# Sparse attention and a capped mixture of experts in one kernel: causal selects queued ahead of folds on GpSimd, gate softmax queued behind the next exponentials, and a new order at the start

## The chip, the cores and the metric

The kernel runs on one core of a Trainium2 chip. The metric is the device time of one execution in microseconds, here the median of three runs. A profiled execution of the same kernel gives the trace.

## The reference

The input is attention for 4 batches of 8 heads, 768 positions and a head width of 64, followed by a mixture of 8 experts over the 3072 x 512 rows that the attention gives.

```python
k_min, k_max = min / max of k over chunks of 32 positions      # 24 chunks
ub = sum_d max(q * k_min, q * k_max)                           # bound per query and chunk
ub = where(own or earlier chunk, ub, -1e9)
sel = chunks that hold the 6 largest ub of the query
scores = where(sel and key <= query, q @ k.T / 8, -1e9)
x = softmax(scores) @ v                                        # heads side by side: 3072 x 512
logits = x @ w_gate;  expert = argmax;  gate = its softmax value
for each of 8 experts: keep the 80 tokens of largest gate that chose it
    out[token] = gate * (relu(x[token] @ w1) @ w2)             # all other rows are zero
```

## The kernel before, in words

The attention works on 16 pairs of heads, four for each batch; all attention matmuls are float32. A small scheduler, `Sync`, records what each operation reads and writes and adds the semaphore waits. Each engine runs its operations in the order in which the program issues them, so the order of the text is the order of five queues: TensorE ("pe"), ScalarE ("act"), VectorE ("dve"), GpSimd ("gp", which also issues the loads of the expert weights) and SP, which issues the other loads and stores.

The main loop at line 633 goes over the pairs. For pair i it issues, in this order: `scores(i)`; at the first pair of a later batch `gate_T` of the batch before; `bounds(i+1)`; `transposes(i+2)`; `values(i)`; `unselT(i+1)`; `rows(i)`; `sums(i)`; `scale_rows(i)`; and, at the last pair of a batch, `gate` and `gate_digits`. Rounds of a top-80 search (`rounds`, a largest-8 search and a removal on VectorE) are scattered between these from pair 4 on.

`transposes` (line 422) turns q and k of a pair with TensorE into the two halves of the score memory SC0 and SC1, copies q and its positive part with ScalarE (qT, rq), copies k with VectorE (kT) and takes the minimum and maximum of each chunk there; GpSimd subtracts them. `bounds` (444) computes the bound of each query and chunk on TensorE and the mask of the chunks that are not selected on VectorE. `unselT` (470) turns that mask.

`scores` (477) goes through six strips of the score matrix, listed in `STEPS`. For a strip TensorE computes the scores and adds the mask, in SC0 and SC1 by turns; ScalarE takes the exponential into EXB (line 497); GpSimd zeroes the entries above the diagonal in the strip's diagonal block (`affine_select`, line 502, called a select here); and GpSimd then folds the strip into ES, a sum over key blocks from which the softmax's denominators are taken (`tensor_tensor`, line 511, called a fold here). The table `ADDS` says which folds follow which strip's select. Before the change strips 1 and 2 have one fold each, strips 3 and 4 three each, strip 5 one. The two selects of strips 4 and 5 therefore stand behind folds in GpSimd's queue.

`values` (514) multiplies the strips with v into OB, in two halves. Its last matmuls in each half need the selects of strips 4 and 5. ScalarE copies OB to oT (526), `rows` (545) turns oT back, and `sums` (528) computes the gate's logits from oT (line 532) and then the denominators from ES (line 537), so this second part needs all folds. `scale_rows` (550) divides and stores the rows.

`gate` (564) reduces the logits of a batch on VectorE, takes one small exponential on ScalarE (line 574) and finishes the softmax and the choice on VectorE (line 582 is its last step). `gate_T` (585) turns the result with TensorE.

Ahead of the loop, lines 355 to 408 issue the first loads and set up constants, among them copies of the gate weights on VectorE (line 407); then `transposes(0)`, `bounds(0)`, `transposes(1)`, `unselT(0)`, with the loads for pairs 2 and 3 between. After the loop follow the last gate, the last search, the choice of slots, and the experts.

Of the kernel before, what the change touches and what calls it, by code (L numbers as in the profile page):

```python
# [17 lines left out]
class Sync:  # L18
# [53 lines left out]
    def op(self, ekey, fn, r=(), w=(), dsem=None, inc=True):  # L72
        is_dma = ekey in self.dma
        stream = self.stream.get(ekey, ekey)
        semkey = dsem if is_dma else ekey
        self.sem(semkey)
        clock = self.clock.setdefault(stream, {})
        need = {}

        def want(ev, same_ok):  # L80
            sk, val = ev
            if sk == ekey and same_ok:
                return
            need[sk] = max(need.get(sk, 0), val)

        for res in r:
            for sk, val in self.lw.get(res, {}).items():
                want((sk, val), ekey == "pe")
        for res in w:
            for sk, val in self.lw.get(res, {}).items():  # L90
                want((sk, val), ekey == "pe")
            for sk, val in self.lr.get(res, {}).items():
                want((sk, val), not is_dma)
        todo = [(sk, v) for sk, v in need.items() if clock.get(sk, 0) < v]

        todo.sort(key=lambda e: -len(self.snaps[e[0]][-1][1]) if self.snaps[e[0]] else 0)
        keep = []
        for i, ev in enumerate(todo):
            implied = False
            for j, other in enumerate(todo):  # L100
                if j == i:
                    continue
                c = {}
                self._learn(c, other)
                if c.get(ev[0], 0) >= ev[1] and not (j > i and self._implied(ev, other)):
                    implied = True
                    break
            if not implied:
                keep.append(ev)
        for ev in keep:  # L110
            assert ev[1] <= self.cnt[ev[0]], (ekey, ev, self.cnt[ev[0]])
            self.queue[ekey].wait_ge(self.sems[ev[0]], ev[1])
        for ev in todo:
            self._learn(clock, ev)
        inst = fn()
        step = 16 if is_dma else 1
        val = self.cnt[semkey] + step
        if inc or is_dma:
            inst.then_inc(self.sems[semkey], step)
            self.cnt[semkey] = val  # L120
            self.snaps[semkey].append((val, dict(clock)))
        for res in w:
            self.lw[res] = {semkey: val}
            self.lr[res] = {}
        for res in r:
            d = self.lr.setdefault(res, {})
            d[semkey] = max(d.get(semkey, 0), val)
        return inst
# [19 lines left out]
def bass_quest_chunk_select__then__topk_capacity_drop_kernel(  # L148
# [26 lines left out]
    def ts(i, n=128):  # L175
# [12 lines left out]
    DIAG = [0, 0, 0, 256, 0, 0]  # L188

    ADDS = [  # L190
        [], [(1, 0, 128, 512)], [(2, 0, 256, 512)], [(3, 0, 512, 768), (3, 256, 512, 768), (1, 384, 512, 640)],
        [(4, 0, 384, 512), (4, 128, 512, 768), (4, 384, 640, 768)], [(5, 0, 640, 768)],
    ]

    FIRST = {(1, 0): (0, 128), (3, 0): (2, 256)}
# [7 lines left out]
    with ExitStack() as pers:  # L203
# [18 lines left out]
        with nc.Block() as blk:  # L222

            @blk.sync
            def _body(_unused):
# [139 lines left out]
                v128 = iv(128, [1, 128])  # L365
                op("gp", lambda: gp.iota(v128, pattern=[[-1, 128]], base=0, channel_multiplier=1), w=["ti"])
                op("dve", lambda: ve.tensor_scalar(ident_f[:], v128, 0, None, ALU.is_equal), r=["ti"], w=["ident_f"])
                for j in range(2):
                    op("dve", lambda: ve.memset(kmm[j][:], 0.0), w=[f"kmm{j}", f"kmd{j}"])
                op("dve", lambda: ve.memset(uns[:], 0.0), w=["uns"])  # L370
# [17 lines left out]
                op("gp", lambda: gp.iota(vr, pattern=[[0, NT], [-1, E]], base=E, channel_multiplier=0),  # L388
                   r=["ti", "ind0", "ind1"], w=["ti"])
                op("dve", lambda: ve.tensor_copy(rank_c[:], vr), r=["ti"], w=["rank_c"])  # L390
                op("dve", lambda: ve.tensor_copy(ident_bf[:], ident_f[:]), r=["ident_f"], w=["ident_bf"])
                op("dve", lambda: ve.memset(ones8[:], 1.0), w=["ones8"])

                vi = iv(128, [1, CAP])
# [7 lines left out]
                op("dve", lambda: ve.tensor_copy(idc[:, :, 0], iv(128, [1, TOKT])), r=["ti"], w=["idc0"])  # L402
                op("gp", lambda: gp.iota(iv(128, [1, TOKT]), pattern=[[0, TOKT]], base=1, channel_multiplier=1), r=["ti"], w=["ti"])
                op("dve", lambda: ve.tensor_copy(idc[:, :, 1], iv(128, [1, TOKT])), r=["ti"], w=["idc1"])
                for h in range(2):
                    pr = slice(h * 64, h * 64 + 64)
                    op("dve", lambda: ve.tensor_copy(wg[pr, :, h * E:(h + 1) * E], wgr[pr, :, :]), r=["wg", f"wgr{h}"], w=[f"wg{h}"])
                WG = ["wg0", "wg1"]

                def wload(e, part):  # L410
# [8 lines left out]
                def pair_of(t, n):  # L419
                    return bass.AP(t, 0, [[2 * n, 128], [n, 2], [1, n]])  # L420

                def transposes(i):
                    s, j = i % NB, i % 2
                    for nm, src, ps in (("qn", qn, 0), ("kn", kn, 1)):
                        for t in range(NT):
                            a = bass.AP(src[s], t * 2 * D, [[2 * NT * D, 128], [1, 2 * D]])
                            op("pe", lambda: pe.transpose(SC[ps][:, ts(t)], a, ident_f[:]),  # L427
                               r=[f"{nm}{s}0", f"{nm}{s}1", "ident_f"], w=[f"SC{ps}"], inc=(t == NT - 1))
                    op("act", lambda: ac.activation(qT[j][:], SC[0][:, 0:S], ACTF.Copy), r=["SC0"], w=[f"qT{j}"])  # L429
                    op("act", lambda: ac.activation(rq[:], SC[0][:, 0:S], ACTF.Relu), r=["SC0"], w=["rq"])  # L430
                    op("dve", lambda: ve.tensor_copy(kT[j][:], SC[1][:, 0:S]), r=["SC1"], w=[f"kT{j}"])
                    kv = bass.AP(kT[j], 0, [[S, 128], [CHUNK, NCH], [1, CHUNK]])
                    op("dve", lambda: ve.tensor_reduce(kmm[j][:, 0, 0:NCH], kv, AX, ALU.min), r=[f"kT{j}"], w=[f"kmm{j}"])
                    op("dve", lambda: ve.tensor_reduce(kmx[:], kv, AX, ALU.max), r=[f"kT{j}"], w=["kmx"])
                    op("gp", lambda: gp.tensor_tensor(kmm[j][:, 1, 0:NCH], kmx[:], kmm[j][:, 0, 0:NCH], ALU.subtract),
                       r=[f"kmm{j}", "kmx"], w=[f"kmd{j}"])

                def stripes(t, off, row, lo, n):

# [145 lines left out]
                def gate_T(b):  # L585
                    for t in range(NT):
                        op("pe", lambda: pe.transpose(OB[0:E, ts(t)], gv[:, b * NT + t, :], ident_f[:]),
                           r=[f"gv{b}", "ident_f"], w=["O0" if t < 4 else "O1"], inc=(t in (3, NT - 1)))
                    op("act", lambda: ac.activation(cand[:, CAP:CAP + S], OB[0:E, 0:S], ACTF.Copy), r=["O0", "O1"], w=["cand"])  # L589
# [34 lines left out]
                        if m < ROUNDS:  # L624
                            top_round(m, False)

                transposes(0)
                load(2, "qk")
                bounds(0)
                transposes(1)  # L630
                load(3, "qk")
                unselT(0)
                for i in range(NP):
                    scores(i)
                    if i % NPB == 0 and i:
                        gate_T(i // NPB - 1)
                    if i + 1 < NP:
                        bounds(i + 1)
                    if i + 2 < NP:
                        transposes(i + 2)  # L640
                    if i + 4 < NP:
                        load(i + 4, "qk")
                    rounds(i, 0, 1)
                    values(i)
                    if i + 2 < NP:
                        load(i + 2, "v")
                    if i + 1 < NP:
                        unselT(i + 1)
                    rounds(i, 1, 2)
                    if i < NP - 1:  # L650
                        wload(i // 2, i % 2)
                    rows(i)
                    sums(i)
                    scale_rows(i)
                    if i % NPB == NPB - 1:
                        gate(i // NPB)
                        if i < NP - 1:
                            gate_digits(i // NPB)
                    rounds(i, 2, 3)
                    if i % 3 == 2 and i < 12:  # L660
                        zk = f"w1_{E - 1}"
                        zr = bass.AP(w1s[E - 1], 0, [[DB * Fd, 128], [1, 2 * Dm]])
                        if i == 2:
                            op("dve", lambda: ve.memset(zr, 0.0), w=[zk])
                        g = i // 3
                        zs = bass.AP(w1s[E - 1], 0, [[DB * Fd, 128], [0, NT], [1, 2 * Dm]]).bitcast(F32)
                        zd = bass.AP(out.tensor, out.offset + g * NT * 128 * Dm, [[Dm, 128], [128 * Dm, NT], [1, Dm]])
                        op("sp", lambda: sp.dma_start(zd, zs), r=[zk], w=[f"outz{g}"], dsem=f"d_zero{g}")


                b = B - 1
                gate_T(b)
                gate_digits(b)
                wload(E - 1, 1)
# [151 lines left out]
```

## Time and profile before

| | |
|---|---|
| runs | 391.44 us median of 3 (391.4 to 392.28) |
| profiled execution | 393.25 us, its span 391.5 us |
| granted TensorE clock, mean | 0.913 |
| TensorE matmul busy | 299.9 us, 77% |
| VectorE busy | 222.6 us, 57% |
| GpSimd busy | 233.0 us, 60% |
| ScalarE busy | 148.5 us, 38% |

The span is the time from the first to the last instruction of the profiled execution, and all times of rows count from its start. The shares are means over stages that differ: the start up to 22 us, sixteen pairs up to 317 us, the last search and the slots up to 358 us, and the experts. In the rows PE is TensorE, PEld its weight loads, ACT ScalarE, DVE VectorE, POOL GpSimd, SP the sync engine; L502 is line 502 of the kernel.

### The profile page before, as it was taken

To read this page: it belongs to the slowest core of one execution; us is meant where nothing else is said; L and a number is where in the kernel's file an instruction comes from. 1 tells how busy PE (TensorE), PEld (TensorE's weight loads), DVE (VectorE), ACT (ScalarE), POOL (GpSimd) and SP (SyncE) were. 2 spreads that over 40 slices of the span, in tenths; PEclk is the share of its full clock that TensorE was granted. 3 is DMA by queue.
4 is the path that set the end of the run, shared out by engine and by line. 5 is a ranking of instruction groups with operands and counts; after the bars stand their busy time and mean duration, and the time that the engine had idled before them with its cause. 6 is when DMAs were issued, how large, how long until landed. Compare 5 with 4: busy or idle time off the path is not lost.

```text
span 391.5 us, 7778 instructions
## 1 busy us (share of the span) xinstructions
PE 299.9 (77%) x3204; PEld 181.5 (46%) x3204; DVE 222.6 (57%) x591; ACT 148.5 (38%) x202; POOL 233.0 (60%) x313
## 2 busy tenths in 40 slices
PE   2198989897888989879989898888979640024994
PEld 2165555454545455546555454545445420014772
DVE  3344244453596776656785865596864058981342
ACT  3064537261735445435636271726434200001220
POOL 4039586685859595939586775768594960005422
PEclk9689999999999999989999999999998885555898
DMA  9843959698578699594989686935556071001121
GB/s 177 146 82 81 167 121 146 129 282 155 102 142 167 102 287 171 103 164 88 192 238 151 128 159 106 264 75 100 82 90 115 14 105 22 1 0 39 46 62 52
DMA packets 104964, 47.50 MB, mean 121 GB/s; under 512 B 88955, under 2 KB 97269, under 8 KB 104928
## 3 DMA queue, kind: packets, MB, share of 16 engines
q1 hardware_dynamic: 89920, 27.94, 30.8%
q0 software_dynamic: 13440, 18.67, 29.6%
q10 hardware_dynamic: 1568, 0.39, 0.5%
q8 instruction: 25, 0.41, 0.4%
q14 instruction: 11, 0.09, 0.1%
HBM read 53.10 MB, written 10.75 MB: 163 GB/s over the span
## 4 chain that ended last, share of the span: by engine, by line
POOL 41%; PE 31%; issue 12%; ACT 6%; DVE 3%; SPq 3%; DMA 1%; POOLq 0%
POOL ES L511 33%; PE SC L486 8%; POOL EXB L502 7%; PE OB L522 5%; ACT EXB L497 5%; PE OB L770 4%; PE OB L547 4%; PE SC L755 3%; PE M L537 3%; SPq L353 2%; PE M L532 2%; PE SC L492 2%; ACT oT L526 2%; PE SC L427 1%; DMA wgr<-in_moe_w_gate_dram 1%
## 5 line engine op out<-in xcount | busy, mean ns | idle before, releaser
L511 POOL TENSOR_TENSOR ES<-ES,EXB 128x256 f32<-128x256 f32 (+1 forms) x112 | 106.9, 961 | 7.8
L486 PE MATMUL SC<-qT,kT 64*128 64x512 f32 (+3 forms) x512 | 98.6, 473 | 8.2 <-ACT EXB L497 6.5
L497 ACT ACTIVATE EXB<-SC 128x1024 f32<-128x1024 f32 x96 | 85.9, 915 | 48.5 <-PE SC L492 46.9
L522 PE MATMUL OB<-EXB,vn 128*64 128x256 f32 (+2 forms) x704 | 81.0, 374 | 22.1 <-POOL EXB L502 22.1
L522 PEld LDWEIGHTS OB<-EXB,vn 128*64 128x64 f32 x704 | 45.9, 141 | 54.9 <-POOL EXB L502 35.0
L486 PEld LDWEIGHTS SC<-qT,kT 64*128 64x128 f32 x512 | 41.7, 190 | 48.3 <-ACT EXB L497 32.2
L511 POOL TENSOR_TENSOR ES<-EXB 128x768 f32<-128x768 f32 (+1 forms) x32 | 49.3, 1541 | 2.7
L526 ACT ACTIVATE oT<-OB 128x512 f32<-128x512 f32 (+1 forms) x32 | 15.7, 490 | 84.0 <-PE OB L522 84.0
L502 POOL TENSOR_SCALAR_AFFINE_SELECT ES<-EXB 128x256 f32<-128x256 f32 x16 | 6.4, 401 | 61.1 <-ACT EXB L497 60.9
L608 DVE MAX8 top<-cand 8x8 f32<-8x848 f32 (+1 forms) x40 | 40.2, 1006 | 1.9 <-ACT cand L589 1.3
L455 DVE STREAM_TRANSPOSE M<-M 128x160 f32<-128x160 f32 x16 | 5.8, 365 | 61.9 <-PE MB L451 61.9
L492 PE MATMUL SC<-unsT,ind 64*128 64x384 bf16 (+3 forms) x256 | 39.3, 300 | 0.0
L502 POOL TENSOR_SCALAR_AFFINE_SELECT EXB<-EXB 128x256 f32<-128x256 f32 x80 | 33.1, 413 | 10.1 <-ACT EXB L497 10.1
L540 DVE STREAM_TRANSPOSE M<-M 128x192 f32<-128x192 f32 x16 | 6.3, 397 | 57.3 <-PE M L537 57.3
L610 DVE MATCH_REPLACE8 cand<-top,cand 8x848 f32<-8x848 f32 (+1 forms) x36 | 35.7, 992 | 0.0
L736 POOL DMA_INDIRECT qn<-x_rows,idx x4 | 3.9, 980 | 36.0 <-issue 36.0
L429 ACT ACTIVATE qT<-SC 128x768 f32<-128x768 f32 x16 | 13.0, 810 | 25.5 <-PE SC L427 25.5
L427 PE MATMUL SC<-ident_f,qn 128*128 128x128 f32 x96 | 15.1, 298 | 8.0 <-DMA qn<-in_q_dram 6.2
L492 PEld LDWEIGHTS SC<-unsT,ind 64*128 64x128 bf16 x256 | 13.1, 96 | 14.5 <-issue 11.3
L427 PEld LDWEIGHTS SC<-ident_f,qn 128*128 128x128 f32 x96 | 11.2, 150 | 12.6 <-issue 10.9
L776 POOL DMA_INDIRECT out_dram<-EXB,idx x8 | 7.4, 921 | 15.9 <-DVE EXB L774 12.9
L747 ACT ACTIVATE rq<-MB 128x320 bf16<-128x320 bf16 x4 | 1.7, 437 | 39.4 <-PE MB L744 39.4
(139 smaller groups left out, 429.0 us busy)
## 6 DMA issues: line engine op xcount, KB each, us to landing
w1s<-in_moe_w_dram POOLq DMA_DIRECT2D x8, 1024.0 KB, 10.1
w2s<-in_moe_w_dram POOLq DMA_DIRECT2D x7, 1024.0 KB, 11.2
qn<-in_q_dram SPq DMA_DIRECT2D x32, 192.0 KB, 3.4
vn<-in_v_dram SPq DMA_DIRECT2D x32, 192.0 KB, 3.9
out_dram<-w1s SPq DMA_DIRECT2D x4, 1536.0 KB, 10.8
kn<-in_k_dram SPq DMA_DIRECT2D x30, 192.0 KB, 3.7
x_rows<-xp SPq DMA_DIRECT2D x16, 192.0 KB, 6.8
EXB<-in_moe_w_dram POOLq DMA_DIRECT2D x1, 1024.0 KB, 9.8
```

The costliest lines, as they stand in the source:

```text
L427: op("pe", lambda: pe.transpose(SC[ps][:, ts(t)], a, ident_f[:]), r=[f"{nm}{s}0", f"{nm}{s}1", "ident_f"], w=[f"SC{ps}"], inc=(t == NT - 1))
L486: op("pe", lambda: pe.matmul(o, kT[j][pr, ts(kt)], qT[j][pr, q0:q1], start=True, stop=False), r=[f"kT{j}", f"qT{j}"], w=[f"SC{s}"], inc=False)
L492: op("pe", lambda: pe.matmul(o, ind[pr, ts(kt)], unsT[j][pr, b0 - 128:q1 - 128], start=False, stop=True), r=[f"ind{h}", f"unsT{j}"], w=[f" ...
L497: op("act", lambda: ac.activation(Ex(st, None, 0, W), src, ACTF.Exp, scale=SCALE), r=[f"SC{s}"], w=[f"E{st}"])
L502: op("gp", lambda: gp.affine_select(ad, a, pattern=[[0, 2], [1, 128]], compare_op=ALU.is_ge, fill=0.0, base=0, channel_multiplier=-1), r=[ ...
L511: op("gp", lambda: gp.tensor_tensor(o, in0, in1, ALU.add), r=[f"E{s2}", f"E{first[0]}"] if first else [f"E{s2}"] + kt, w=kt)
L522: op("pe", lambda: pe.matmul(OB[pr, q0:q1], vn[s][:, kt, h, :], ex, start=(n == 0), stop=last), r=[f"vn{s}{h}", "ES0" if st is None else f ...
L526: op("act", lambda: ac.activation(oT[:, q0:q1], OB[:, q0:q1], ACTF.Copy), r=[f"O{bk}"], w=[f"oT{bk}"])
L547: op("pe", lambda: pe.transpose(OB[:, ts(t)], oT[:, ts(t)], ident_f[:]), r=["oT0", "oT1", "ident_f"], w=[f"O{t // 4}"], inc=(t in (3, NT - ...
L608: op("dve", lambda: ve.max(dst, cv), r=["cand"], w=[f"top{int(last)}{n}"])
L610: op("dve", lambda: ve.match_replace(cv, dst, cv, -2.0), r=["cand", f"top{int(last)}{n}"], w=["cand"])
L770: op("pe", lambda: pe.matmul(o, hTv(e)[:, fb * CAP:(fb + 1) * CAP], w2v(e)[:, fb, :], start=(fb == 0), stop=(fb == FB - 1)), r=[f"hT{s}{fb ...
```

## The change

It has three parts. In `ADDS` the seven folds of strips 3 to 5 are listed with strip 5, so that GpSimd gets the selects of strips 3, 4 and 5 right behind the fold of strip 2, and the seven folds after the last select. `gate` and `gate_digits` of a batch are no longer issued at the end of its last pair, but in the next pair, behind `scores` and ahead of `gate_T`. For the last batch `gate` is issued after the loop.

At the start the bf16 copy of the identity is made earlier, 40 matmuls on it whose result nothing reads are issued on TensorE ahead of the first transposes, `transposes` is split into four functions, the second pair's transposes and its copy of q are issued ahead of the first pair's bounds, and the copies of the gate weights come after `unselT(0)`.

```diff
     ADDS = [
-        [], [(1, 0, 128, 512)], [(2, 0, 256, 512)], [(3, 0, 512, 768), (3, 256, 512, 768), (1, 384, 512, 640)],
-        [(4, 0, 384, 512), (4, 128, 512, 768), (4, 384, 640, 768)], [(5, 0, 640, 768)],
+        [], [(1, 0, 128, 512)], [(2, 0, 256, 512)], [], [],
+        [(3, 0, 512, 768), (3, 256, 512, 768), (1, 384, 512, 640), (4, 0, 384, 512), (4, 128, 512, 768),
+         (4, 384, 640, 768), (5, 0, 640, 768)],
     ]
...
                 op("dve", lambda: ve.tensor_scalar(ident_f[:], v128, 0, None, ALU.is_equal), r=["ti"], w=["ident_f"])
+                op("dve", lambda: ve.tensor_copy(ident_bf[:], ident_f[:]), r=["ident_f"], w=["ident_bf"])
...
-                for h in range(2):
-                    pr = slice(h * 64, h * 64 + 64)
-                    op("dve", lambda: ve.tensor_copy(wg[pr, :, h * E:(h + 1) * E], wgr[pr, :, :]), r=["wg", f"wgr{h}"], w=[f"wg{h}"])
...
-                transposes(0)
+                def warm(n):
+                    for _ in range(n):
+                        op("pe", lambda: pe.matmul(OB[:, 0:128], ident_bf[:], ident_bf[:], start=True, stop=True),
+                           r=["ident_bf"], w=["O0"], inc=False)
+
+                warm(40)
+                turn_q(0)
+                take_q(0)
+                take_r(0)
+                take_k(0)
                 load(2, "qk")
+                turn_q(1)
+                take_q(1)
+                load(3, "qk")
                 bounds(0)
-                transposes(1)
-                load(3, "qk")
+                take_r(1)
+                take_k(1)
                 unselT(0)
+                for h in range(2):
+                    pr = slice(h * 64, h * 64 + 64)
+                    op("dve", lambda: ve.tensor_copy(wg[pr, :, h * E:(h + 1) * E], wgr[pr, :, :]), r=["wg", f"wgr{h}"], w=[f"wg{h}"])
                 for i in range(NP):
                     scores(i)
+                    if i % NPB == 0 and i:
+                        gate(i // NPB - 1)
+                        gate_digits(i // NPB - 1)
                     if i % NPB == 0 and i:
                         gate_T(i // NPB - 1)
...
-                    if i % NPB == NPB - 1:
-                        gate(i // NPB)
-                        if i < NP - 1:
-                            gate_digits(i // NPB)
...
                 b = B - 1
+                gate(b)
                 gate_T(b)
```

`turn_q` holds the transposes of q and k on TensorE, `take_q` and `take_r` the two ScalarE copies of q, and `take_k` the VectorE copy of k, its minima and maxima, and GpSimd's difference.

## Rows read from the trace of the kernel before

**Rows 1.** Page, chain that ended last: shares of the span by engine.
```profile
POOL 41%; PE 31%; issue 12%; ACT 6%; DVE 3%; SPq 3%; DMA 1%; POOLq 0%
```

**Rows 2.** Chain of waits in pair 5, 114 to 133: start us, us, what.
```profile
114.37 1.06 PE SC L486 x4
...
117.82 0.42 POOL EXB L502
...
129.85 0.39 ACT oT L526
...
131.62 0.65 PE M L537 x16
```

**Rows 3.** Timeline, pair 5: start us, us, engine, line, operation, [idle before, its releaser].
```profile
120.64 1.30 ACT L497 ACTIVATE EXB<-SC 128x1024 f32<-128x1024 f32 x2 [0.39 <-PE SC L492]
...
123.24 0.44 PE L522 MATMUL OB<-ES,vn 128*64 128x128 f32 x4
...
126.13 2.60 PE L522 MATMUL OB<-EXB,vn 128*64 128x128 f32 x28 [0.73 <-POOL EXB L502]
...
128.88 0.40 POOL L502 TENSOR_SCALAR_AFFINE_SELECT EXB<-EXB 128x256 f32<-128x256 f32 x1
...
129.37 0.72 POOL L511 TENSOR_TENSOR ES<-ES,EXB 128x256 f32<-128x256 f32 x1
```

**Rows 4.** Waits of TensorE, 22.4 to 320: us in total, times, longest.
```profile
PE OB L522 <- POOL EXB L502: 22.1, 28, 3.1
```

**Rows 5.** Timeline, pair 4, in which the first batch's gate is computed.
```profile
94.30 1.13 PE L486 MATMUL SC<-qT,kT 64*128 64x512 f32 x4
...
97.63 0.24 ACT L574 ACTIVATE lgx<-lg 128x48 f32<-128x48 f32 x1 [4.63 <-DVE lg L573]
...
98.66 0.21 DVE L582 TENSOR_TENSOR gv<-oh,gt 128x48 f32<-128x48 f32 x1
...
98.84 1.13 PE L486 MATMUL SC<-qT,kT 64*128 64x512 f32 x4 [2.17 <-ACT EXB L497]
...
99.77 0.58 POOL L502 TENSOR_SCALAR_AFFINE_SELECT EXB<-EXB 128x256 f32<-128x256 f32 x1 [0.50 <-ACT EXB L497]
```

**Rows 6.** Timeline, pair 8, in which the second batch's gate is computed.
```profile
172.54 1.34 PE L486 MATMUL SC<-qT,kT 64*128 64x512 f32 x4 [2.17 <-ACT EXB L497]
...
178.06 0.82 PE L587 MATMUL OB<-ident_f,gv 128*8 128x128 f32 x6
...
180.97 0.44 PE L522 MATMUL OB<-ES,vn 128*64 128x128 f32 x4
...
185.81 0.38 ACT L526 ACTIVATE oT<-OB 128x256 f32<-128x256 f32 x1 [1.78 <-PE OB L522]
```

**Rows 7.** Timeline, the start up to the first scores.
```profile
6.24 1.51 PE L427 MATMUL SC<-ident_f,qn 128*128 128x128 f32 x6 [6.24 <-DMA qn<-in_q_dram]
...
14.17 0.44 DVE L407 COPY wg<-wgr 64x32 f32<-64x32 f32 x2 [5.04 <-DMA wgr<-in_moe_w_gate_dram]
...
21.05 0.41 DVE L467 TENSOR_TENSOR uns<-M,top 128x240 bf16<-128x240 f32 x1
...
21.69 0.74 PE L473 MATMUL MB<-ident_bf,uns 128*128 128x128 bf16 x5
...
22.36 1.50 PE L486 MATMUL SC<-qT,kT 64*128 64x512 f32 x4
```

**Rows 8.** DMA issues under way between 6.5 and 7.4: KB each, us to landing.
```profile
kn<-in_k_dram SPq DMA_DIRECT2D x1, 192.0 KB, 5.4
```

**Rows 9.** Stretch of pair 6: us, busy of each engine, granted clock, DMA share, GB/s.
```profile
132.30:150.20 17.90, 16.12 (x177) 9.41 (x177) 12.91 (x31) 8.56 (x11) 12.93 (x17) 1.00 0.99 224
```

**Rows 10.** Timeline, the last two pairs.
```profile
291.59 4.27 PE L522 MATMUL OB<-EXB,vn 128*64 128x128 f32 x32 [2.41 <-POOL EXB L502]
...
298.28 1.13 PE L486 MATMUL SC<-qT,kT 64*128 64x512 f32 x4
...
317.01 0.40 DVE L540 STREAM_TRANSPOSE M<-M 128x192 f32<-128x192 f32 x1 [12.86 <-PE M L537]
```

More of the change, by code (lines that the diff above doesn't have):

```diff
@@ L390, in _body @@
                 op("dve", lambda: ve.tensor_copy(rank_c[:], vr), r=["ti"], w=["rank_c"])
-                op("dve", lambda: ve.tensor_copy(ident_bf[:], ident_f[:]), r=["ident_f"], w=["ident_bf"])
                 op("dve", lambda: ve.memset(ones8[:], 1.0), w=["ones8"])
@@ L420, in pair_of, with turn_q @@
                     return bass.AP(t, 0, [[2 * n, 128], [n, 2], [1, n]])
-                def transposes(i):
-                    s, j = i % NB, i % 2
+                def turn_q(i):
+                    s = i % NB
                     for nm, src, ps in (("qn", qn, 0), ("kn", kn, 1)):
@@ L428, in transposes, with take_q, take_r, take_k @@
                                r=[f"{nm}{s}0", f"{nm}{s}1", "ident_f"], w=[f"SC{ps}"], inc=(t == NT - 1))
+                def take_q(i):
+                    j = i % 2
                     op("act", lambda: ac.activation(qT[j][:], SC[0][:, 0:S], ACTF.Copy), r=["SC0"], w=[f"qT{j}"])
+                def take_r(i):
                     op("act", lambda: ac.activation(rq[:], SC[0][:, 0:S], ACTF.Relu), r=["SC0"], w=["rq"])
+                def take_k(i):
+                    j = i % 2
                     op("dve", lambda: ve.tensor_copy(kT[j][:], SC[1][:, 0:S]), r=["SC1"], w=[f"kT{j}"])
@@ L436, in transposes @@
                        r=[f"kmm{j}", "kmx"], w=[f"kmd{j}"])
+                def transposes(i):
+                    turn_q(i)
+                    take_q(i)
+                    take_r(i)
+                    take_k(i)
                 def stripes(t, off, row, lo, n):
```

## The prediction

> **What bounds the kernel now.** I read the chain of waits first: 41% of its span is GpSimd work and 31% TensorE, and its largest single entry is the folds of line 511 [rows 1]. Between start and tail the kernel repeats one pair of heads 16 times, so I took one plain pair, pair 5, apart. On the chain its first score matmul is at 114.37 and the next pair's at 131.62 + 0.65 = 132.27, a period of 17.90 us; GpSimd enters at 117.82 with its second select [rows 2].
>
> The timeline of the same pair shows what that queue holds back. The two last exponentials start at 120.64 and take 1.30, so the last strip is ready at 121.94; its select ends at 128.88 + 0.40 = 129.28, because folds stand ahead of it. TensorE came to the value matmuls at 123.24 and stopped in front of them twice; the last fold ends at 129.37 + 0.72 = 130.09 [rows 3]. Over all pairs TensorE waited 22.1 us, in 28 waits, with value matmuls for selects [rows 4]. So the loop is closed not by GpSimd's amount of work but by the place of the last select in it.
>
> **The change, part by part.** The profiled execution took 393.25 us with a span of 391.5; the runs' median is 391.44, 1.8 lower. I work out a difference on the trace and take it off both.
>
> *Selects ahead of folds.* GpSimd gets the same six selects and nine folds, seven of them now behind the last select. From 117.82 its queue has no hole, so the last fold still ends at 130.09, 15.72 us after the pair's start [rows 2, 3]. The last select loses six folds ahead of it (the seventh stood behind it before): three of the size that takes 0.72 [rows 3] and three twice as wide, by estimate 1.3, together 6.1 us. So it will end at 129.28 - 6.1 = 123.2, when TensorE arrives at 123.24, so the value matmuls run unbroken. Their unbroken length is in the trace: in pair 8, where TensorE came late, they started at 180.97 and the ACT copy of their result at 185.81, 4.84 later [rows 6]. In the plain pair: values at 123.24 - 114.37 = 8.87 after the start, copy at 13.71; from the copy to the sums' second half, which reads the folds, 131.62 - 129.85 = 1.77 [rows 2], so TensorE is there at 15.48. It waits for the last fold, 15.72 + 0.05 = 15.77, takes 0.65, and the next pair starts at 16.42. Late next is thus the last fold, with TensorE 0.3 us behind it. Gain 1.48 us per plain pair.
>
> Bounds: were the folds no limit, 15.48 + 0.65 = 16.13. From the other side, TensorE is busy 16.12 us of such a stretch of 17.90 [rows 9]; if all of that were work (some is pipelined waiting) and of its idle time only the 0.73 before the 28 matmuls [rows 3] went, 17.17. I take 16.42, since its terms are rows of this stage.
>
> *Count.* From the first pair's scores at 22.36 to the last's at 298.28 there are 15 periods, 275.9 us [rows 7, 10]: three in which a batch's gate is computed (20.0 each, by pair 4, 94.30 to the 114.3 above [rows 5]) and 12 others, 215.9. Those after: 12 x 16.42 + 0.5 for the first, whose clock is low, = 197.5. Gain 18.4.
>
> *The gate behind the next pair's exponentials.* Before, the small exponential (97.63) stood on ACT ahead of the next pair's six and waited for VectorE's scaling and reductions; TensorE's scores then waited 2.17 us [rows 5]. That stall goes and another comes: TensorE's transposes of the gate stand behind the scores and ahead of this pair's bounds, transposes and values, and now wait for the small exponential, which waits for the sixth large one. It can start 121.94 - 114.37 = 7.6 after the pair's start; VectorE's last gate step ends 98.66 + 0.21 - 97.63 = 1.24 later, so the gate's transposes start at 8.9, where TensorE arrives at about 6.5. From there the values are 2.91 away (178.06 to 180.97), the copy 4.84 more: 16.65 [rows 5, 6]; with 1.77 and 0.65, 19.1. VectorE has the gate's digits ahead of its bounds work, but the bounds matmuls come behind the gate's transposes too, so nobody waits for that. A gate period goes from 20.0 to 19.1, 3 x 0.9 = 2.7, and what ends last in it is TensorE, no longer the folds.
>
> The clock counts in these three places, since TensorE idles 2.4 us. Of two equal waits of 2.17 us before, one (98.84) was followed by four score matmuls in 1.13 us, the other (172.54) by the same four in 1.34; and after 2.41 us in pair 14 32 value matmuls took 4.27 [rows 5, 6, 10], where 48 took 4.84. One such drop costs between 4.27 - 32/48 x 4.84 = 1.0 and half of 4.27 = 2.1 where TensorE is on the path. I charge 2.0 for the three together; bounds 0 and 6.3. The Trainium skill (TensorE: Matmul & The Clock Gate, Part 1) says that the clock is throttled by default, released by activity, and that its monitor runs freely, so that equal gaps can fall either way; the trace agrees, with one drop behind two waits of 2.17. By that rule the charge differs from run to run.
>
> *First two pairs, weights, dummy matmuls.* VectorE stood idle for 5.04 us until 14.17 for the gate weights, whose two copies (0.44) are ahead of the first kT copy [rows 7]. They move behind the second pair's kT work; the sums of pair 0 are the first to need them. So the kT copy starts when VectorE's setup is done, 14.17 - 5.04 = 9.13, plus 0.2 for the identity copy now ahead in it: 9.3 instead of 14.6. From there to the mask of unselected chunks it was 21.05 + 0.41 - 14.6 = 6.9, so the mask is there at 16.2. The first scores came 0.9 behind it (22.36), partly behind the second pair's transposes, which are through by now; I take 0.6: 16.8. Gain 5.6.
>
> What moves ahead of it: the second pair's transposes, before the first pair's bounds on TensorE. They need that pair's keys; the last of these transfers was issued by 6.5 at the latest and took 5.4 [rows 8], so landed by 11.9, and six transposes at the start's 1.51 [rows 7] end by 13.4, where the bounds could start at about 12.5. So that costs between nothing and 0.9; nothing, if it was issued before 6. The 40 dummy matmuls start near 1.7 and are free until the queries land at 6.24. By the nearest row, five bf16 transposes of the same size in 0.74 [rows 7], they take 5.9 and end at 7.6; if each cost the 0.25 of the float32 ones, 10 us and 11.7. The first pushes the first transposes by 1.4, which the setup up to 9.3 hides nearly; the second costs 4. I take the first, the price nearest to it in kind. Bounds for the start's gain: 1.5 to 6.2. The loads of pairs 2 and 3 stand in SP's queue behind the same transfers as before.
>
> *Last pair.* From 298.28 to the sums' end at 317.01 it took 18.7 [rows 10]; with the selects ahead it ends like a plain one, 16.4, plus 0.4 since TensorE idles before the last fold and may run its last matmuls slowly: gain 1.9. The 74.5 us of tail behind it hold nothing that changes.
>
> **Sum.** 18.4 + 2.7 - 2.0 + 5.6 + 1.9 = 26.6. 393.25 - 26.6 = 366.7 for a profiled execution, 391.44 - 26.6 = 364.8 for the median.
>
> **Rivals.**
> (a) *The gate's stall sets the low clock each time*, through transposes and values: up to 1.5 on the 2.91 and 2.1 on the values, about 3 each, 9 instead of 2.0: 371.8. For it: three idle stretches as long as the one that dropped in pair 14. Against: one of the two waits of 2.17 did not.
> (b) *TensorE becomes the bound of the plain pair*: halfway to 17.17, 12 x 0.4 = 5: 370. For it: 0.3 us of slack. Against: 8.87 and 4.84 hold its waits already.
> (c) *Transfers become the bound* in the four pairs that also zero the output: the DMA engines are 0.99 busy of 17.90 us [rows 9], 17.7 for a period of 16.4. If someone waited, 4 x 1.3 = 5: 370. Against: queries, keys and values are asked for about two pairs ahead, so 1.3 us can spill over.
> (d) *Only the start gains*: the sums' wait for the folds takes what the selects' wait gives. The folds would have to end at 17.2 instead of 15.72: about 386.
> (e) *Slower*: the folds, now in one block, lie beside other VectorE steps and lengthen. That decides from 26.6 / 16 = 1.7 us per pair on 6.1 + 0.72 = 6.8 us, a quarter; at the stretch of the one select beside the gate's VectorE steps, 0.58 against 0.40 [rows 3, 5], 45%, it is 3.1 per pair: 391.4 + 16 x 1.4 = 414. Against: GpSimd folds without a hole in exactly this stretch already, beside the same VectorE steps, so what they cost is in the 15.72. The Trainium skill (GPSIMD Engine Reference, Specifications) states that GpSimd's SBUF interfaces are shared with VectorE and contend with instructions of two SBUF inputs; the long select agrees, the folds don't show it.
>
> **How the numbers follow.** Forecast (360 to 368.5) 0.62; (a) 0.14; (b) 0.10; (c) 0.04; (d) 0.05; (e) 0.03; no change, because the start gives back what the pairs win, 0.02. Range: at the best the start gains 6.2, no clock drops and four plain pairs reach 16.13, 391.44 - 30.4 = 361; small gains beside them are possible, so 359.5. Above, (a) to (c) are taken in: 373. Faster by over 0.3% (about what a measurement of this kernel tells from no change, 1.2 us) 0.95, within it 0.02, slower 0.03.
>
> **What would show it.** Right: scores 16.4 us apart in plain pairs; no wait of value matmuls for selects; the sums' second half waiting for the last fold; first scores near 16.8; gate transposes waiting some 2.4 us in pairs 4, 8 and 12. Wrong: a last fold later than 15.9 after the pair's start, value matmuls longer than 4.9 us in plain pairs, a low granted clock there, or a first kT copy later than 10.5.

## The result and the profile after

The changed kernel takes 370.09 us (median of four runs, 369.75 to 375.59), the kernel before beside it 391.73: ratio 0.944, 95% interval 0.9425 to 0.9462. One of the four runs, the 375.59, showed a lower granted clock (0.898, the others 0.915 to 0.920), and the ratio is taken without it. The profiled execution took 370.24 with a span of 368.5, so the trace is 23.0 us shorter where the medians are 21.6 apart; the profiled execution of before was 1.5 above its median. The page's chain by engine has hardly changed [rows 1]:

```profile
POOL 40%; PE 34%; issue 12%; ACT 7%; DVE 4%; DMA 1%; POOLq 0%
```

A plain pair, pair 5, in the timeline (start us, us, engine, line, operation, [idle before, its releaser]); it answers to [rows 2, 3]:

```profile
105.20 1.13 PE L498 MATMUL SC<-qT,kT 64*128 64x512 f32 x4
...
112.68 1.13 POOL L514 TENSOR_SCALAR_AFFINE_SELECT EXB<-EXB 128x256 f32<-128x256 f32 x3
...
114.14 0.44 PE L534 MATMUL OB<-ES,vn 128*64 128x128 f32 x4
114.41 4.49 PE L534 MATMUL OB<-EXB,vn 128*64 128x384 f32 x44
115.12 5.61 POOL L523 TENSOR_TENSOR ES<-ES,EXB 128x512 f32<-128x512 f32 x6
...
120.79 0.48 PEld L549 LDWEIGHTS M<-ES,onc 128*32 128x32 f32 x16 [0.42 <-POOL ES L523]
```

The three last selects end at 113.81, 8.6 after the pair's start, before the value matmuls, which run as one block of 48. What TensorE waits for now is the last fold (115.12 + 5.61 = 120.73), for 0.42 us, ahead of the second half of the sums. The stretch of pair 5 (us, busy of each engine, granted clock, DMA share, GB/s) answers to [rows 9]; the chain's next pair starts 16.4 us after this one:

```profile
105.20:121.60 16.40, 15.91 (x181) 9.51 (x177) 12.97 (x32) 8.55 (x11) 12.80 (x17) 1.00 0.77 159
```

TensorE's waits from 16.8 to 295 (us in total, times, longest) answer to [rows 4]. The 22.1 us for selects are gone; a new line of 10 us in three waits has come, in the three gate pairs:

```profile
PE OB L599 <- DVE gv L594: 10.0, 3, 3.4
PE M L549 <- POOL ES L523: 4.3, 3, 2.4
```

Pair 4, the first gate pair, in the timeline, answers to [rows 5, 6]:

```profile
83.53 1.13 PE L498 MATMUL SC<-qT,kT 64*128 64x512 f32 x4
...
91.05 0.24 ACT L586 ACTIVATE lgx<-lg 128x48 f32<-128x48 f32 x1
...
92.10 1.26 POOL L523 TENSOR_TENSOR ES<-EXB 128x512 f32<-128x512 f32 x1
...
92.42 1.01 DVE L594 TENSOR_TENSOR gv<-oh,gt 128x48 f32<-128x48 f32 x1
...
93.44 5.75 POOL L523 TENSOR_TENSOR ES<-ES,EXB 128x512 f32<-128x512 f32 x6
93.48 0.82 PE L599 MATMUL OB<-ident_f,gv 128*8 128x128 f32 x6 [3.34 <-DVE gv L594]
93.54 1.18 DVE L607 TENSOR_TENSOR gdf<-gt,gsp 128x6 f32<-128x6 f32 x1
...
95.47 1.54 PE L425 MATMUL SC<-ident_f,qn 128*128 128x128 f32 x6
...
98.01 0.44 PE L534 MATMUL OB<-ES,vn 128*64 128x128 f32 x4
```

Two things are to be seen. The product gv on VectorE, 0.21 us before, takes 1.01: it starts at 92.42 inside the fold of 92.10 and ends at 93.43, just behind the fold's end at 93.36. The difference gdf, for the gate's digits, does the same with the next fold. Two shorter steps ahead of gv, beside the three selects, took 0.38 and 0.40 where 0.21 and 0.16 stood before. And TensorE's transposes behind the wait take 1.54 for six, where they take 0.87 at full clock: the granted clock of this stretch is 0.92, in plain pairs 1.00. The pair lasts 21.7 us (83.53 to 105.20); in pair 8 the wait is as long but the clock holds. The stretches of the two pairs, then the rows of pair 8:

```profile
83.50:105.20 21.70, 18.11 (x186) 11.41 (x182) 16.82 (x44) 9.48 (x13) 13.24 (x18) 0.92 0.72 118
...
154.40:174.40 20.00, 16.40 (x185) 10.00 (x181) 15.23 (x42) 9.48 (x13) 13.23 (x18) 1.00 0.67 118
```

```profile
164.33 0.82 PE L599 MATMUL OB<-ident_f,gv 128*8 128x128 f32 x6 [3.36 <-DVE gv L594]
...
165.78 0.87 PE L425 MATMUL SC<-ident_f,qn 128*128 128x128 f32 x6
...
167.24 0.44 PE L534 MATMUL OB<-ES,vn 128*64 128x128 f32 x4
```

The start answers to [rows 7], the last pair to [rows 10]:

```profile
6.32 0.84 PE L425 MATMUL SC<-ident_f,qn 128*128 128x128 f32 x6 [0.35 <-DMA qn<-in_q_dram]
...
9.30 0.95 DVE L437 COPY kT<-SC 128x768 f32<-128x768 f32 x1
...
16.80 2.08 PE L498 MATMUL SC<-qT,kT 64*128 64x512 f32 x4
...
277.95 1.13 PE L498 MATMUL SC<-qT,kT 64*128 64x512 f32 x4
...
293.51 1.51 PE L549 MATMUL M<-ES,onc 128*32 128x192 f32 x16 [2.41 <-POOL ES L523]
...
295.08 0.40 DVE L552 STREAM_TRANSPOSE M<-M 128x192 f32<-128x192 f32 x1 [11.26 <-PE M L549]
```

### The profile page after: what moved, and what is told of

The parts are those of the page before. It is cut to its first block, busy times and chain, and to the rows that moved or that the text cites. A ratio compares the mean times of both kernels' runs of the same rounds, so it can differ in the third digit from the quotient of the medians.

```text
span 368.5 us, 7857 instructions
## 1 busy us (share of the span) xinstructions
PE 297.6 (81%) x3244; PEld 183.4 (50%) x3244; DVE 231.2 (63%) x591; ACT 149.3 (41%) x202; POOL 231.8 (63%) x313
## 4 chain that ended last, share of the span: by engine, by line
POOL 40%; PE 34%; issue 12%; ACT 7%; DVE 4%; DMA 1%; POOLq 0%
POOL ES L523 32%; PE SC L498 10%; ACT EXB L509 7%; POOL EXB L514 6%; PE OB L534 5%; PE OB L797 4%; PE M L549 4%; PE SC L782 3%; PE SC L504 2%; PE SC L425 2%; PE M L463 1%; PE OB L559 1%; DVE gv L594 1%; DMA kn<-x_rows,idx 1%; PE OB L599 1%
## 5 line engine op out<-in xcount | busy, mean ns | idle before, releaser
L534 PE MATMUL OB<-EXB,vn 128*64 128x256 f32 (+2 forms) x704 | 71.9, 360 | 0.0
L498 PEld LDWEIGHTS SC<-qT,kT 64*128 64x128 f32 x512 | 40.9, 188 | 42.4 <-ACT EXB L509 26.4
L534 PEld LDWEIGHTS OB<-EXB,vn 128*64 128x64 f32 x704 | 46.7, 137 | 23.0 <-issue 10.0
L514 POOL TENSOR_SCALAR_AFFINE_SELECT EXB<-EXB 128x256 f32<-128x256 f32 x80 | 31.0, 407 | 10.7 <-ACT EXB L509 10.7
L549 PE MATMUL M<-ES,onc 128*32 128x192 f32 x256 | 14.3, 343 | 5.0 <-POOL ES L523 4.3
L714 PE MATMUL M<-dg,ones 8*128 8x8 f32 x2 | 0.6, 367 | 20.9 <-DVE dg L712 20.9
```

Of the source, the lines that this page charges most:

```text
L498: op("pe", lambda: pe.matmul(o, kT[j][pr, ts(kt)], qT[j][pr, q0:q1], start=True, stop=False), r=[f"kT{j}", f"qT{j}"], w=[f"SC{s}"], inc=False)
L514: op("gp", lambda: gp.affine_select(ad, a, pattern=[[0, 2], [1, 128]], compare_op=ALU.is_ge, fill=0.0, base=0, channel_multiplier=-1), r=[ ...
L534: op("pe", lambda: pe.matmul(OB[pr, q0:q1], vn[s][:, kt, h, :], ex, start=(n == 0), stop=last), r=[f"vn{s}{h}", "ES0" if st is None else f ...
L549: op("pe", lambda: pe.matmul(M0[c * 32:c * 32 + 32, 0:192], onc[:, h, :], stripes(ES, h * S + c * 32, 0, 0, None), start=False, stop=(h == ...
```

## The experiments

Four kernels ran on each of three chips. On the second and third the kernel before took 397.9 and 396.6 us where the first gave 392.2. The traces taken there show some 5 us more in the experts at the end: in the changed kernel's, 78.4 us from the last sums to the end and not 73.5. So ratios and stretches of the trace are compared, not times across chips. Times are medians; the interval of the ratio to before stands beside them.

**The gate back in its old place.**

```diff
                     scores(i)
-                    if i % NPB == 0 and i:
-                        gate(i // NPB - 1)
-                        gate_digits(i // NPB - 1)
...
                     scale_rows(i)
+                    if i % NPB == NPB - 1:
+                        gate(i // NPB)
...
```

> The changed kernel with the gate back at the end of a batch's last pair; folds and start as changed. In the changed kernel the gate pairs last 21.7, 20.1 and 21.6 us where 19.1 was forecast. Theory A (new gate place is the loss: TensorE waits 3.35 us for VectorE, and the low clock follows): with the gate back, GpSimd's chain of 16.4 is delayed by the 2.1 us that the exponentials start late, so gate pairs last 18.5 and the run is 3 x 2.6 = 7.8 faster than the changed kernel, about 362.3. Rival B (the move was a gain, and the gate pairs are long for a reason that both places share, such as transfers or the top-80 rounds): gate pairs stay at 21 or longer, 370 to 373.

366.27 us, ratio 0.934 (0.932 to 0.937): faster than the changed kernel, by 3.8, not 7.8. The gate pairs last 20.4, 18.75 and 18.75, together 5.5 less. One of them lost 1.6 to the clock, as the first row shows (2.03 us for four score matmuls, 1.13 in pair 8), and in the last pair low-clock scores took 1.7 of the gain. Theory A holds in its place and sign; in size it came to half. In the timeline:

```profile
88.14 2.03 PE L498 MATMUL SC<-qT,kT 64*128 64x512 f32 x4 [2.17 <-ACT EXB L509]
...
157.48 0.21 DVE L594 TENSOR_TENSOR gv<-oh,gt 128x48 f32<-128x48 f32 x1
157.65 1.13 PE L498 MATMUL SC<-qT,kT 64*128 64x512 f32 x4 [2.17 <-ACT EXB L509]
```

gv is at 0.21 again: at this place in the pair GpSimd has no fold to run.

**The gate behind strip 1's exponential.**

```diff
                         op("act", lambda: ac.activation(Ex(st, None, 0, W), src, ACTF.Exp, scale=SCALE),
                            r=[f"SC{s}"], w=[f"E{st}"])
+                        if st == 1 and after:
+                            after()
...
-                    scores(i)
+                    scores(i, gates if i % NPB == 0 and i else None)
```

`gates` issues `gate` and `gate_digits` of the batch before.

> The changed kernel with the gate issued inside scores, behind the exponential of strip 1 instead of behind strip 5. VectorE's inputs are there about 3.3 us after the pair's start, and ACT has a hole of 0.39 us between the exponentials of strips 1 and 2 that takes the small one. Theory A (only the place on ACT's queue made TensorE wait): the gate's transposes find their input ready at 6.5, gate pairs last 16.7 to 17, run about 357. Rival C (VectorE's gate steps are held up by GpSimd's folds wherever they stand): the steps run beside the fold of strip 1 (1.81 us) and end up to 2 us later, gate pairs 17.5 to 18.5, 359.5 to 362.

357.62 us, ratio 0.912 (0.910 to 0.914), 12.5 us below the changed kernel. All three gate pairs last 16.64. In the timeline of pair 4:

```profile
83.25 1.13 PE L498 MATMUL SC<-qT,kT 64*128 64x512 f32 x4
...
86.61 0.23 ACT L588 ACTIVATE lgx<-lg 128x48 f32<-128x48 f32 x1
...
87.27 1.81 POOL L525 TENSOR_TENSOR ES<-EXB 128x768 f32<-128x768 f32 x1
...
87.62 1.53 DVE L596 TENSOR_TENSOR gv<-oh,gt 128x48 f32<-128x48 f32 x1
...
89.79 0.82 PE L601 MATMUL OB<-ident_f,gv 128*8 128x128 f32 x6
...
99.89 1.13 PE L498 MATMUL SC<-qT,kT 64*128 64x512 f32 x4
```

Rival C is right that the fold holds gv up (1.53 us, until 89.15, behind the fold that ends at 89.08) and wrong on the price: TensorE is still at the scores, and the gate's transposes start at 89.79 without a wait.

**Dummy matmuls in the gate's wait.**

```diff
                         gate_digits(i // NPB - 1)
+                        warm(30)
                     if i % NPB == 0 and i:
                         gate_T(i // NPB - 1)
```

> The changed kernel with 30 more dummy matmuls on TensorE ahead of each gate_T, which fill some 2 to 2.7 us of its wait of 3.35 us. Theory (low clock behind the wait costs 1.6 us in pairs 4 and 12, where twelve transposes took 2.54 and not 1.5): in all three gate pairs the transposes of q take 0.87 and not 1.54, pairs 4 and 12 last 20.0 like pair 8, run 3.2 faster: 366.9. Rival (the transposes there are slow because of something else than the clock, such as VectorE's or ACT's reads): no change, 370.

368.7 us (367.02 to 369.77), ratio 0.9415 (0.938 to 0.945): the interval does not part it from the changed kernel. The trace does: the remaining wait is 1.57, the transposes of q take 0.88 in pair 4, and all three gate pairs last 20.06 where 21.7, 20.1 and 21.6 stood. The profiled execution, 367.02, is 3.2 us shorter than that of the changed kernel, as was forecast, so the theory on the clock holds in this trace. The four runs differ by up to 2.7 us among themselves, the slower ones have no trace, and what sets them apart stays open. In the timeline:

```profile
90.11 1.85 PE L641 MATMUL OB<-ident_bf 128*128 128x128 bf16 x30
...
93.53 0.82 PE L599 MATMUL OB<-ident_f,gv 128*8 128x128 f32 x6 [1.57 <-DVE gv L594]
...
94.98 0.88 PE L425 MATMUL SC<-ident_f,qn 128*128 128x128 f32 x6
```

**The gate's reciprocal in PSUM.**

```diff
-                gt6 = al(pers, "gt6", [128, NT])
+                gt6 = SC[1][:, 1000:1000 + NT]
```

> The changed kernel with the gate's reciprocal kept in PSUM (a free corner of SC1) and not in SBUF, so that the product gv and the difference gdf read one operand from SBUF and one from PSUM. Theory (a VectorE instruction with two SBUF inputs waits until the running GpSimd fold ends: gv took 1.01 and not 0.21, gdf 1.18 and not 0.29): gv takes 0.2 to 0.3 and the gate's transposes start 0.8 earlier, 2.3 us in the run, 367.8, and more if the shorter wait keeps the clock up; the steps that still read two SBUF operands stay long. Rival (GpSimd's folds slow every VectorE instruction, or the time is the order of the queue): gv stays at 1.0, 370.

369.38 us (366.22 to 370.94), ratio 0.940 (0.934 to 0.945), no difference that the runs can tell; the steps are decided by the trace:

```profile
92.64 1.26 POOL L523 TENSOR_TENSOR ES<-EXB 128x512 f32<-128x512 f32 x1
92.73 0.20 DVE L593 RECIPROCAL SC<-lsum 128x6 f32<-128x6 f32 x1
92.97 0.20 DVE L594 TENSOR_TENSOR gv<-oh,SC 128x48 f32<-128x48 f32 x1
...
93.23 1.44 PE L599 MATMUL OB<-ident_f,gv 128*8 128x128 f32 x6 [2.56 <-DVE gv L594]
...
93.98 5.74 POOL L523 TENSOR_TENSOR ES<-ES,EXB 128x512 f32<-128x512 f32 x6
94.06 1.33 DVE L611 TENSOR_TENSOR RC<-oh,idc 128x96 bf16<-128x96 f32 x1
```

With one operand in PSUM gv takes 0.20 in the middle of a fold, and the wait is 2.56, 0.8 shorter; RC, a later product of the gate that still reads two SBUF operands, takes 1.33 and not the 0.25 that it takes beside no fold. So it is the operand's place and not the queue's order. In the profiled execution the time did not follow since the low clock came in all three gate pairs (1.44 us for six transposes that take 0.82 in pairs 4 and 12, a step later in pair 8), which lasted 20.7, 20.9 and 20.7.

**Each part alone, on the kernel before.** The diffs are the three parts of the change itself.

> The kernel before with nothing changed but the order of GpSimd's selects and folds. Theory (the folds' part is worth 1.5 us in 12 plain pairs and 1.5 in the gate pairs and the last, whatever the start does): 392 - 18.4 - 1.6 - 0 to 4 = 368 to 372; as the kernel with the gate back took 366.3 and holds the start's 5.6 besides, 371.9. Plain pairs 16.4 apart, first scores at 22.4. Rival (the parts lean on each other, for instance the pairs get their transfers in time only because the start is earlier): plain pairs above 17, 378 or more.

374.58 beside 397.87, ratio 0.944 (0.941 to 0.947): 23.3 us less. Plain pairs are 16.4 apart, first scores at 22.4, the gate pairs 18.7. So the folds' part doesn't lean on the start: 0.944 times the start's 0.990 below is 0.935, and the kernel with both and the old place of the gate had 0.934.

> The kernel before with nothing changed but the place of the gate, behind the next pair's exponentials. Theory (the gate's transposes then hold TensorE until 9.8 after the pair's start, the values end 7.8 later): gate pairs 20.0, at low clock 21.6, against 20.0 before, so no gain, 391.5 to 396. Rival (the removed stall of 2.1 us is worth something where TensorE must wait for the late selects anyway): gate pairs 17.9, 386.

405.98, ratio 1.023 (1.019 to 1.026): 8.1 us slower, twice the theory's worst. The gate pairs last 22.4, 23.6 and 22.4, together 8.1 more than before. In the changed kernel the same place cost 3.8, so this part does lean on the folds' order. With folds between the selects, two VectorE steps are held up, not one:

```profile
102.44 1.26 POOL L511 TENSOR_TENSOR ES<-EXB 128x512 f32<-128x512 f32 x1
102.50 1.23 DVE L580 TENSOR_SCALAR lsum<-lsum 128x6 f32<-128x6 f32 x1
...
103.78 2.06 POOL L511 TENSOR_TENSOR ES<-ES,EXB 128x512 f32<-128x512 f32 x2
103.99 1.12 DVE L582 TENSOR_TENSOR gv<-oh,gt 128x48 f32<-128x48 f32 x1
...
105.16 1.23 PE L587 MATMUL OB<-ident_f,gv 128*8 128x128 f32 x6 [4.09 <-DVE gv L582]
```

> The kernel before with nothing changed but the start. Theory: first scores at 16.8 and not 22.4, all else as before: 392 - 5.6 = 386.4. Rival (the loads of pairs 2 and 3 or the weights come later against the pairs, and pairs 0 to 2 give some of it back): 388 to 391.

393.61, ratio 0.990 (0.987 to 0.993): 4.3 us less. First scores at 16.6, 5.8 earlier; the second pair's come 4.7 earlier than before, since pair 0 lasts 1 us longer, at a granted clock of 0.55 from 16 to 20 us. That is less than the theory's 5.6, near the rival's 1 to 4.

**Without the 40 dummy matmuls.** The diff removes `warm(40)`. It ran twice, the second time beside the changed kernel.

> The changed kernel without the 40 dummy matmuls. Theory (VectorE's setup, which ends at 9.3, sets the first kT copy, and not TensorE): the first transposes take 1.5 for six and not 0.84 but still end by 9.3, first scores at 16.8 to 17.5, 370 to 371. Rival (the dummies hold TensorE's clock through the start): bounds, mask transposes and pair 0 slower, first scores after 18, 372 or more.

> The changed kernel once more, unchanged, as the measure for the other three on one chip. Ratio to the kernel before 0.943 to 0.946; first scores at 16.3 to 16.9 with the low clock (four matmuls in 2.0 us), gate pairs 20.0 to 21.7.

> The changed kernel without the 40 dummy matmuls, beside the changed kernel on the same chip. Theory W (the dummies only shift by chance where TensorE's clock falls; VectorE's setup sets the start): same as the changed kernel within 1 us. Rival X (the dummies cost: with them the first scores ran at low clock in all six traces, 2.01 us for four matmuls, and without them at full clock, 1.06, and the second pair's scores came 2 us earlier): 1.5 to 2 us faster than the changed kernel. Rival Y (they help): slower by 1 or more.

First run: 376.19, ratio 0.951 (0.945 to 0.957). Second: 378.42, ratio 0.951 (0.947 to 0.956), beside the changed kernel's 375.70, ratio 0.950 (0.945 to 0.956). The medians lie 2.7 us apart, but the six runs of each spread over 374.8 to 379.2 and 374.8 to 380.3, so no difference can be measured. The first trace had the first scores at full clock at 16.00 (four in 1.13 us), which made rival X; the second had them at 16.17 in 2.08, as with dummies, and X falls. In both the first kT copy starts at 9.29, as with dummies, because VectorE's setup sets it.

**Gate behind strip 1, and constants set up later; with and without dummies.**

```diff
-                op("dve", lambda: ve.memset(ones8[:], 1.0), w=["ones8"])
... (to idc1, moved into late())
                     scale_rows(i)
+                    if i == 0:
+                        late()
```

> The changed kernel with the gate behind the exponential of strip 1, and with the constants that nobody reads before pair 4 set up behind pair 0 and not ahead of the first kT copy. Theory: gate pairs 16.7, worth 12.5 against the changed kernel; kT copy at 7.9 and not 9.3, first scores 1.4 earlier at 15.4: together 13.9 us less than the changed kernel, ratio to before about 0.908. Rival (the second pair's keys land too late for an earlier start, at up to 11.9): the start gains nothing, 12.5 less, 0.912; or GpSimd's small operations behind pair 0 delay pair 1 by about 1.

> The same without the 40 dummy matmuls. Theory: the first transposes, 1.5 us for six, then set the kT copy (9.1), so the late setup gains nothing, but the first pair's scores may run at full clock; against the former between 1 us slower and 1 us faster. Rival X of the run without dummies says 0.5 to 1 faster; if dummies help once the setup no longer hides the transposes, 1 to 2 slower.

361.94 with dummies, ratio 0.912 (0.910 to 0.915); 362.55 without, 0.9125 (0.910 to 0.915). Beside the changed kernel on this chip that is 13.8 and 13.2 less; the first is what was expected, but not from the start: the ratio is that of the run without the later setup. The kT copy came at 8.07 and the first scores at 15.04, 1.2 earlier than in that run (16.3), yet pair 0 lasted 18.5 where 17.8 stood, at a granted clock of 0.50 from 16 to 20 us. Pair 1 lasted 16.8: GpSimd's index operations stand in its queue and wait for VectorE, and its first select starts 3.6 after the pair's start where 2.5 is usual:

```profile
33.58 1.13 PE L485 MATMUL SC<-qT,kT 64*128 64x512 f32 x4
...
36.05 0.23 POOL L639 IOTA tmp_i<- 128x128 int32 x1 [1.96 <-DVE iota L638]
...
37.15 0.41 POOL L503 TENSOR_SCALAR_AFFINE_SELECT ES<-EXB 128x256 f32<-128x256 f32 x1
...
50.37 1.13 PE L485 MATMUL SC<-qT,kT 64*128 64x512 f32 x4
```

Without dummies the copy came at 9.15 and the first scores at 16.11, as its theory had it: in these traces, where the setup no longer hides the transposes, the dummies bring the start forward by 1.1 us, but the two times can't be told apart. So what counts is the gate behind strip 1's exponential: 0.912 of the time before, with the later setup or without it.

## Why the prediction was right, and where it was off

364.8 was forecast, 370.09 came: 5.3 above, inside the range of 359.5 to 373, but outside the 360 to 368.5 that got 0.62. The range held it because rivals (a) to (c) had been taken in. The sign and most of the gain came from the folds' part and the start, as forecast; the gate's part had the wrong sign, a gain of 0.7 forecast and a loss of 3.2 in the trace. Of the signs of being wrong none came (last fold 15.5 after the pair's start, values 4.8 long, first kT copy at 9.30); of those of being right one was off, as the gate's transposes waited 3.3 and not 2.4. Step by step on the trace, where 26.6 was forecast and 23.0 came:

- *Selects ahead of folds*: right. Plain pairs were to last 16.42, and do 16.4; the 12 of them take 197.8 where 197.5 stood. The last fold ends last, TensorE waits 0.42 for it where 0.3 was worked out. Alone this part is worth 23.3 us between the medians (5.6% by the ratio).
- *First two pairs*: right in size, 5.6 at the first scores (16.80). That the setup hides the dummies held too; 4.3 of it is left in the run of this part alone, as pair 0 runs at low clock.
- *The gate*: wrong, and it is the step that failed. 3 x 0.9 gained less 2.0 for the clock was forecast, 59.3 us for the three pairs; they took 63.35, 3.2 more than the 60.2 of before. Two terms were mis-sized. The 1.24 from the small exponential to VectorE's last gate step was read where GpSimd stood idle; beside selects and folds it is 2.4 (91.05 to 93.43, 0.8 of the difference in gv), so the gate's transposes start at 9.95 after the pair's start instead of 8.9, three times 1.05. And the low clock took 1.6 in two of the pairs (4.5 from the gate's transposes to the values, where 2.91 held in pair 8), 3.2 instead of 2.0. The comparison was off too: 19.1 was set against the 20.0 of before, but with the folds' part alone, and the gate at its old place, the gate pairs last 18.7. So even 19.1 would have been a loss. Sent back alone, the gate's old place was 3.8 us faster, and moved alone it made the kernel before 2.3% slower.
- *The last pair*: 17.1 from its scores to the sums' end, 16.8 forecast. The tail, for which nothing was forecast, came out 1.1 shorter, which is luck.
- *Profiled execution and median*: taken as 1.8 apart for both; the changed kernel's are 0.15 apart, so 1.7 of the 5.3 comes from this and 3.6 from the trace.

Rival (a) is what happened in part: its place was right, its price (9 instead of 2.0) too high for the clock, which took 3.2, and it lacked the hold on VectorE. Rival (e) saw the contention of GpSimd and VectorE but on the wrong side: the folds hardly lengthened (0.965 us in the mean of the 112 of one group, 0.961 before), VectorE's steps did. Its argument against looked at the steps of a plain pair and not at the gate's, which the change itself brings beside the folds. Its sentence on the Trainium skill (GPSIMD Engine Reference, Specifications), on contention with instructions of two SBUF inputs, named the right cause. The trace agrees: gv with two SBUF inputs took 1.01. That one with an operand in PSUM does not wait (0.20) is what the run with the reciprocal in PSUM shows. The 112 folds, before and after:

```profile
L511 POOL TENSOR_TENSOR ES<-ES,EXB 128x256 f32<-128x256 f32 (+1 forms) x112 | 106.9, 961 | 7.8
L523 POOL TENSOR_TENSOR ES<-ES,EXB 128x256 f32<-128x256 f32 (+1 forms) x112 | 106.8, 965 | 6.4
```

Rivals (b), (c) and (d) fell: plain pairs last 16.4.

## What to carry to other kernels

In a queue that is served in order, put what another engine waits for ahead of what only the end needs: the same GpSimd work in another order gave 5.6%. Before moving a short chain of small steps, look at what runs on the neighbouring engine at the new place, not only at the step's duration at the old one. And place a small operation in a hole of its engine's queue (here 0.39 us between two exponentials) rather than ahead of or behind the whole row: with the folds reordered, the gate pairs last 18.7 at full clock with the exponential ahead of the row, 20.1 behind it and 16.6 in the hole, and up to 1.6 more at the low clock at the first two places.

## What the runs showed of the hardware

VectorE does not share with a running GpSimd fold, it waits for the fold's end: gv ends 0.07 us behind the fold in the changed kernel, and 0.07 behind it behind strip 1, whatever is left of the fold when gv starts (0.94 and 1.46). The steps so held read SBUF only: products and differences of two SBUF tensors (0.21 to 1.01, 0.29 to 1.18, 0.25 to 1.33), but also two kinds of one SBUF tensor: a scalar addition (0.16 to 1.23, in the kernel with the gate alone moved) and a cast from SBUF to SBUF (0.18 to 1.14, behind strip 1). Wide reductions (0.95), the reciprocal (0.19) and products with an operand in PSUM (0.20) ran beside folds at their usual length. GpSimd paid a little: the six last folds took 5.75 in pair 4 where 5.61 stands in pair 5; a select beside the gate's products at the old place took 0.58 and not 0.40 [rows 5]; and three selects behind strip 1's gate took 1.29 and not 1.13.

After equal waits of TensorE the granted clock fell in one pair and held in another of the same execution: behind 3.34 to 3.36 us the same transposes took 1.54, 0.87 and 1.54 in the three gate pairs. Which pairs fell was not a matter of one execution: the changed kernel's second trace, on another chip, and the first without dummies show the same pattern (gate pairs of 21.7, 20.05 and 21.7). In the second without dummies pair 8 fell too (22.5), and behind 2.56 all three fell. So the length of the wait alone doesn't give the term of 1 to 2 us; what decides it stays open.
